# One queue for the step B loads of the first batch, and no early group of the second

## The chip, the cores and the metric

The kernel runs on one core of one Trainium2 chip. The metric is device time of one launch in microseconds: the median of three runs of the kernel before is 1350.76 us (1348.87 to 1351.63). Engines are named as the profile names them: PE (TensorE), PEld (its weight load), DVE (VectorE), ACT (ScalarE), POOL (GpSimd), SP (SyncE, which here only issues DMAs).

## The reference

Each of four batches of 3008 rows by 256 columns goes through a real Fourier transform over the rows, a complex linear map with bias, a soft threshold, and the inverse transform. The 12032 resulting rows then go through a two-layer network whose middle has 2048 columns and a leaky rectifier with a slope per column.

```python
X = np.fft.rfft(x, axis=1)
Yr = Xr @ w_r - Xi @ w_i + b_r
Yi = Xr @ w_i + Xi @ w_r + b_i
Yr = np.sign(Yr) * np.maximum(np.abs(Yr) - lam, 0.0)   # lam = 0.01; Yi likewise
y = np.fft.irfft(Y, n=x.shape[1], axis=1)
h = y @ w_in
out = (np.maximum(h, 0.0) + alpha * np.minimum(h, 0.0)) @ w_out
```

## The kernel before

The transform of 3008 = 47 x 64 rows is made of matmuls with tables, in four steps per batch. Step A (`a_mm`, `a_evac`) multiplies 16 groups of rows with the table `lf_s` into 96 partitions, which are 4 blocks by 2 halves by 12 pairs. Step B (`b_load`, `b_mm`) takes one of the 12 pairs: it gathers 4 partitions per half of step A's result into a tile `bt` of 128 partitions, and multiplies it with rows of the table `rb_s`. The mixing (`m_mm`) multiplies with the split weights `wr_s` and `wi_s`, `m_evac` applies bias and threshold, step C (`c_mm`, `c_evac`) multiplies with `cf_s` and stores to a DRAM tensor `zd`. Step D (`d_load`, `d_step`) reads `zd` back and makes the rows that feed the network (`l1_step`, `l2_step`).

The order of the work is written out by hand; every engine runs its instructions in that order, and a tile is reused only when its last reader is done. The first batch runs alone, ahead of the network:

- The opening: SP loads the rows of the first batch; PE runs step A on them, then four groups (0 to 3) of the second batch (`EARLY = 4`), then 70 matmuls of no use on a tile `idle` (`keep_warm(WARM)`) until step B's data is there. The step B loads of the first batch go from SBUF (`a0_s`) to SBUF and are issued by POOL; those of later batches go from DRAM and are issued by SP. Three `bt` tiles rotate, so the load of pair q needs `b_mm` of pair q - 3 to be done.
- The pair loop, t = 0 to 12: step B of pair t, mixing of pair t - 1, step C of pair t - 3. Beside it, `pump` converts the raw network weights (`cw_s`, loaded by SP in pieces of 512 KB, three buffers) into two parts each, on ACT, DVE and POOL; the table `PT` says how many of its steps an iteration takes. SP also loads table rows (`load_rb`) and, in iterations 5 to 9, rows of the second batch (`a_load`); POOL loads the table `cf_s`.
- The tail (`TAIL`): the last steps of the loop, and ten groups of step A of the second batch (4 to 13) that fill PE while `zd` is written and read back. Then the network's steps begin; the first 48 of them also carry the rest of the conversion and the last two groups (14 and 15) of step A of the second batch, at steps 9 and 15.

The lists `A1_TAGS` and `X1_TAGS` only say in which free tile each early group's result and rows are put. `load_mix` loads the raw mixing weights, `split_mix` splits them in two parts (first part on ACT, rest on POOL), `load_tables` loads `rd_s` and `alpha_s`.

Of the kernel before, what the change touches and what calls it, by code (L numbers as in the profile page):

```python
# [93 lines left out]
def fft_mix_moe(ctx, tc, x, w_r, w_i, b_r, b_i, w_in, w_out, alpha, la, rb, lc, rd, lf, cf, sel, out):  # L94
# [41 lines left out]
    def split(src, hi, lo, e_hi, e_lo):  # L136

        if e_hi is A:
            A.activation(out=hi, in_=src, func=AF.Copy)
        else:  # L140
            e_hi.tensor_copy(out=hi, in_=src)
        e_lo.tensor_tensor(out=lo, in0=src, in1=f(hi), op=ALU.subtract)
# [29 lines left out]
    def load_tables():  # L172
        nc.sync.dma_start(out=rd_s, in_=rd)
        nc.sync.dma_start(out=alpha_s, in_=alpha.rearrange("(k p) -> p k", p=128))
# [33 lines left out]
    def load_mix(*tags):  # L208
        for w, tag in zip((w_r, w_i), tags):
            t = work.tile([128, CT, C], F32, tag=tag, name="wm_f", bufs=1 if tag[1] in "tc" else None)  # L210
            nc.sync.dma_start(out=t, in_=w.rearrange("(k p) f -> p k f", p=128))
            mix_w.append(t)

    def load_rb(n0, n1):
        nc.sync.dma_start(out=rb_s[:, n0:n1], in_=rb[:, n0:n1])
# [9 lines left out]

    def split_mix():
        for t, w in zip(mix_w, mix):
            split(t, w[:, 0], w[:, 1], A, G)
        mix_w.clear()

    def combine_mix():
# [109 lines left out]
    def a_load(b, g):  # L341

        if g == 0:
            ad[b] = dram.tile([NQ, R, C], F32, tag="ad", name=f"ad{b}")
        src = x[b].rearrange("(p r) c -> p r c", r=R)[:, 4 * g:4 * g + 4]
        if b == 0:
            ts = [x_s[:, 4 * g:4 * g + 4]]
        elif b == 1 and g in X1_TAGS:
            tags = X1_TAGS[g]
            ts = [work.tile([NP, 4 // len(tags), C], F32, tag=tag, name="xt", bufs={"Yl": None, "gh": 4}.get(tag, 1))  # L350
                  for tag in tags]
        else:
            ts = [work.tile([NP, 4, C], F32, tag="xt", name="xt")]
        if (b, g) == (0, 0):
            ts = [ts[0][:, 0:2], ts[0][:, 2:4]]
        n = 4 // len(ts)
        for i, t in enumerate(ts):

            for p in ((0, 80), (80, NP)):
                nc.sync.dma_start(out=t[slice(*p)], in_=src[slice(*p), n * i:n * i + n])  # L360
        xt[b, g] = ts
# [50 lines left out]
    def b_load(b, q):  # L412
        t = work.tile([128, 2, C], F32, tag="bt", name="bt", bufs=3)
        if b == 0:
            src = a0_s.rearrange("(w s q) g r c -> q w s (g r) c", w=4, s=2)[q]
        else:
            src = ad[b].rearrange("(w s q) r c -> q w s r c", w=4, s=2)[q]

        for k in range(2):
            (nc.gpsimd if b == 0 else nc.sync).dma_start(out=t[:, k], in_=src[:, k])  # L420
        bt[b, q] = t

    def b_mm(b, q):
# [548 lines left out]
    MM, M2 = 2, 4  # L972
    PAT = [0, 0] + [1] * 46
    NG = R // 2
    EARLY = 4
    FILL = 14
    C0 = 2
    PT = [1, 2, 3, 3, 3, 3, 3, 3, 3, 3, 4, 4]
    TAIL = [['me', 1], ['ce', 3], ['cm', 2], ['cm', 1], ['ce', 2], ['ce', 1], ['d'], ['f', 4], ['e'], ['f', 6]]
    WARM = 70  # L980
    A1_TAGS = ("zst", "zst", "Yt", "Yc", "bt", "bt", "bt", "Xh", "Xl", "Xh", "Xl", "zst", "zst", "Yc")
    X1_TAGS = {4: ("Yl", "Yl"), 5: ("os", "Yt"), 6: ("gh",) * 4}
    idle = const.tile([128, 128], BF16, name="idle")

    def keep_warm(n):
# [4 lines left out]
    with tc.manual_schedule():  # L990
# [5 lines left out]
        for g in range(NG // 2):  # L996
            a_load(0, g)
        load_rb(0, 4)
        for g in range(EARLY // 2):
            a_load(1, g)  # L1000
        load_mix("Yh", "Yh")
        load_rb(4, 12)
        conv_tags.update(v1=("yh", "yl"), ex=("xh", "xh"), lf=("xl", "xl"))
        for _ in range(C0):
            conv_load()
        seq = [(0, g) for g in range(NG)] + [(1, g) for g in range(EARLY)]

        for n, (b, g) in enumerate(seq):
            a_mm(b, g)
            if n >= 1:  # L1010
                a_evac(*seq[n - 1])
            if n == NG:
                for q in range(3):
                    b_load(0, q)
                split_mix()
                bias_parts()
        a_evac(*seq[-1])
        half(0)
        put()
        load_tables()  # L1020
        keep_warm(WARM)

        def run(fn, q, *args):
            if 0 <= q < NPAIR:
                fn(0, q, *args)

        a1 = [EARLY]
        hold = []

        def a_fill(n):  # L1030
# [5 lines left out]
        for t in range(NPAIR + 1):  # L1036
            run(b_mm, t)
            run(b_load, t + 3)
            run(c_evac, t - 4)
            run(b_evac, t)  # L1040
            run(m_evac, t - 2)
            run(m_mm, t - 1, ps_h)
            run(b_evac2, t)
            run(c_mm, t - 3)
            if t < NPAIR:
                pump(PT[min(t, len(PT) - 1)])
            if t in (2, 5):
                load_rb(2 * t + 8, 2 * t + 14)
            if t < 8 and t % 2 == 0:
                load_cf(3 * t, 3 * t + 6)  # L1050
            if 5 <= t < 10:
                a_load(1, t - 3)
            if t == 10:
                half(1)
                conv_m[1] = FT
# [199 lines left out]
```

## Time and profile before

| What | Value |
|---|---|
| median of three runs | 1350.76 us |
| profiled execution, its own time | 1350.56 us |
| its span, first to last instruction | 1348.8 us |
| PE, PEld busy share of the span | 99%, 93% |
| DVE, ACT, POOL | 77%, 56%, 28% |
| granted TensorE clock, mean | 0.999 |

Busy shares are means over the whole span. The change touches only the first 190 us or so: the opening (to 30 us), the pair loop with its tail (30 to 101 us), and the first 48 steps of the network. What an edit there is worth has to be read from these stretches. The profile prints a DMA share (mean busy share of the 16 DMA engines) and GB/s for any stretch; a share can pass 1 where transfers overlap on one engine.

### The profile page before, as it was taken

What the parts mean: (1) busy time and instruction counts of PE and PEld (TensorE: products, weight loads), DVE (VectorE), ACT (ScalarE), POOL (GpSimd) and SP (SyncE); (2) the same over time, 40 slices, a digit from 0 to 9 for tenths busy, and PEclk for the clock granted to TensorE, in tenths of its full rate; (3) what the DMA queues carried; (4) which work ended last, traced back from release to release, by engine and by line L of the source; (5) the groups of instructions that cost most, each with busy time, mean ns of one, the idle gap of its engine ahead of it and who ended that gap; (6) DMA issues with size and microseconds to landing.
All of it is one profiled execution on the core that took longest, in us unless ns stands there. A gap on an engine that the chain in (4) does not pass through costs nothing.

```text
span 1348.8 us, 25138 instructions
## 1 busy us (share of the span) xinstructions
PE 1335.5 (99%) x9200; PEld 1250.7 (93%) x9200; DVE 1034.9 (77%) x1938; ACT 761.0 (56%) x1526; POOL 375.5 (28%) x400
## 2 busy tenths in 40 slices
PE   8999999999999999999999999999999999999998
PEld 4979999999999999999999999999999999999998
DVE  2767856776777777776768888888888888888885
ACT  3566655665566645555555555655555555555653
POOL 3864642222321222222221211121112111211222
PEclk9999999999999999999999999999999999999999
DMA  9974223342333312111110110111011101110001
GB/s 236 251 202 140 81 94 106 105 138 74 98 115 112 111 54 79 53 51 47 36 36 2 40 28 4 37 28 28 6 35 28 28 6 35 29 28 8 22 17 29
DMA packets 88119, 89.67 MB, mean 66 GB/s; under 512 B 42317, under 2 KB 70448, under 8 KB 87995
## 3 DMA queue, kind: packets, MB, share of 16 engines
q1 hardware_dynamic: 79700, 77.02, 20.1%
q0 software_dynamic: 5168, 8.02, 2.2%
q10 hardware_dynamic: 3127, 3.01, 0.7%
q8 instruction: 73, 1.20, 0.4%
q14 instruction: 51, 0.42, 0.1%
HBM read 50.49 MB, written 34.34 MB: 63 GB/s over the span
## 4 chain that ended last, share of the span: by engine, by line
PE 89%; DVE 3%; DMA 3%; issue 2%; ACT 1%; SPq 1%; POOL 0%; ACTq 0%; DVEq 0%; POOLq 0%
PE ps_h L794 24%; PE ps_h L689 13%; PE ps_m L491 6%; PE ps_o L895 6%; PE ps_o L896 6%; PE ps_o L894 6%; PE ps_d L620 4%; PE ps_o L728 3%; PE ps_o L727 3%; PE ps_o L726 3%; PE ps_b L428 2%; PE o_last L727 1%; PE o_last L728 1%; PE o_last L726 1%; PE o_last L894 1%
## 5 line engine op out<-in xcount | busy, mean ns | idle before, releaser
L794 PE MATMUL ps_h<-yh,w 128*128 128x512 f32 (+1 forms) x960 | 315.6, 389 | 0.0
L833 POOL TENSOR_TENSOR l<-t,h 128x512 fp32r<-128x512 f32 x98 | 127.0, 1296 | 496.5 <-ACT h L831 456.9
L794 PEld LDWEIGHTS ps_h<-yh,w 128*128 128x128 f32 x960 | 180.0, 188 | 33.2
L798 DVE SCALAR_TENSOR_TENSOR sq<-sq,beta_s,ps_h 128x512 f32<-128x512 f32 (+1 forms) x240 | 167.9, 732 | 54.5 <-ACT sq L797 53.6
L689 PE MATMUL ps_h<-yh,w 128*128 128x384 f32 (+1 forms) x704 | 207.0, 337 | 1.3 <-DVE q L696 1.3
L794 PE MATMUL ps_h<-yl,w 128*128 128x512 f32 (+1 forms) x480 | 186.2, 388 | 0.0
L696 DVE SCALAR_TENSOR_TENSOR q<-q,beta_s,ps_h 128x384 f32<-128x384 f32 (+1 forms) x192 | 115.1, 600 | 91.8 <-ACT q L695 90.9
L700 ACT ACTIVATE gh<-q 128x384 fp32r<-128x384 f32 (+1 forms) x192 | 99.1, 516 | 148.0 <-DVE q L696 145.3
L701 POOL TENSOR_TENSOR gl<-q,gh 128x384 fp32r<-128x384 f32 (+1 forms) x90 | 96.8, 1075 | 274.9 <-ACT gh L700 265.4
L813 ACT ACTIVATE dh<-sq 128x768 fp32r<-128x768 f32 x112 | 94.8, 846 | 117.8 <-DVE sq L798 75.8
L797 ACT ACTIVATE sq<-ps_h 128x512 f32<-128x512 f32 (+1 forms) x240 | 133.2, 586 | 26.9 <-PE ps_h L794 25.6
L689 PEld LDWEIGHTS ps_h<-yh,w 128*128 128x128 f32 x704 | 129.3, 189 | 4.4 <-DVE q L696 1.3
L695 ACT ACTIVATE q<-ps_h 128x384 f32<-128x384 f32 (+1 forms) x192 | 91.9, 479 | 62.1 <-PE ps_h L689 61.4
L831 ACT ACTIVATE h<-t 128x512 fp32r<-128x512 f32 x98 | 62.0, 633 | 105.2 <-DVE t L829 103.0
L689 PE MATMUL ps_h<-yl,w 128*128 128x384 f32 (+1 forms) x352 | 116.5, 331 | 0.0
L728 PE MATMUL ps_o<-w,gl 128*128 128x256 f32 x384 | 108.0, 281 | 0.6 <-POOL gl L701 0.6
L727 PE MATMUL ps_o<-w,gh 128*128 128x256 f32 x384 | 107.8, 281 | 0.0
L726 PE MATMUL ps_o<-w,gh 128*128 128x256 f32 x384 | 107.7, 280 | 0.0
L794 PEld LDWEIGHTS ps_h<-yl,w 128*128 128x128 f32 x480 | 90.5, 189 | 13.6
L828 DVE TENSOR_TENSOR dl<-sq,dh 128x768 fp32r<-128x768 f32 x98 | 93.4, 953 | 3.9 <-ACT dh L813 3.9
L896 PE MATMUL ps_o<-l,sw_a 128*128 128x256 f32 x294 | 82.0, 279 | 0.0
L894 PE MATMUL ps_o<-h,sw_a 128*128 128x256 f32 x294 | 81.9, 279 | 0.0
(214 smaller groups left out, 3618.5 us busy)
## 6 DMA issues: line engine op xcount, KB each, us to landing
zt<-zd SPq DMA_DIRECT2D x32, 384.0 KB
zd<-zst SPq DMA_DIRECT2D x37, 256.0 KB
ad<-ast SPq DMA_DIRECT2D x48, 192.0 KB
bt<-ad SPq DMA_DIRECT2D x72, 128.0 KB
xt<-in_x SPq DMA_DIRECT2D x21, 320.0 KB
out<-oT SPq DMA_DIRECT2D x152, 32.0 KB
cw_s<-in_moe_w_in SPq DMA_DIRECT2D x8, 512.0 KB
cw_s<-in_moe_w_out SPq DMA_DIRECT2D x8, 512.0 KB
```

The source lines that it names most:

```text
L689: PE.matmul(ps, wi_h[m // FH][:, w, ct, 128 * (m % FH):128 * (m % FH) + 128], a[:, ct, 0:n], start=(k == 0), stop=(k == 3 * CT - 1))
L696: V.scalar_tensor_tensor(out=q, in0=q, scalar=beta_s[:, m:m + 1], in1=ps, op0=ALU.mult, op1=ALU.add)
L700: A.activation(out=hi, in_=q, func=AF.Copy)
L726: PE.matmul(a, hi[:, t], w[:, 0], start=(i, k) in first, stop=False)
L727: PE.matmul(a, hi[:, t], w[:, 1], start=False, stop=False)
L728: PE.matmul(a, lo[:, t], w[:, 0], start=False, stop=(i, k) in last)
L794: PE.matmul(ps, wi_h[m // FH][:, w, ct, 128 * (m % FH):128 * (m % FH) + 128], a[:, ct, 0:w1], start=(k == 0), stop=(k == 3 * CT - 1))
L797: A.activation(out=q[:, j], in_=ps, func=AF.Relu, scale=-1.0)
L798: V.scalar_tensor_tensor(out=q[:, j], in0=q[:, j], scalar=beta_s[:, m:m + 1], in1=ps, op0=ALU.mult, op1=ALU.add)
L833: G.tensor_tensor(out=l24, in0=t24, in1=f(h24), op=ALU.subtract)
L894: PE.matmul(o, wh, gh, start=first, stop=False)
L896: PE.matmul(o, wh, gl, start=False, stop=last)
```

## The change

All step B loads of the first batch are issued by SP. The first three pairs' loads stand right behind step A and, but for one load of table rows, ahead of everything else that SP has to issue; the two first loads of raw weights come after them, `load_tables` in iteration 6. The rest of the mixing weights' split moves from POOL to DVE, behind the bias. No group of the second batch runs in the opening: the tail fills PE with groups 0 to 9 (ten, as before), whose rows are loaded in iterations 7 to 11, and groups 10 to 15 run at steps 9, 15, 21, 27, 33 and 39 of the network. `WARM` goes from 70 to 65, and `PT` from 1 and 2 conversion steps in the first two iterations to 0 and 3 (35 in all, as before).

```diff
     def split_mix():
         for t, w in zip(mix_w, mix):
-            split(t, w[:, 0], w[:, 1], A, G)
+            split(t, w[:, 0], w[:, 1], A, V)
...
         for k in range(2):
-            (nc.gpsimd if b == 0 else nc.sync).dma_start(out=t[:, k], in_=src[:, k])
+            nc.sync.dma_start(out=t[:, k], in_=src[:, k])
...
-    EARLY = 4
-    FILL = 14
+    FILL = 10
...
-    PT = [1, 2, 3, 3, 3, 3, 3, 3, 3, 3, 4, 4]
+    PT = [0, 3, 3, 3, 3, 3, 3, 3, 3, 3, 4, 4]
...
-    WARM = 70
...
+    WARM = 65
...
         for g in range(NG // 2):
             a_load(0, g)
         load_rb(0, 4)
-        for g in range(EARLY // 2):
-            a_load(1, g)
         load_mix("Yh", "Yh")
+        conv_tags.update(v1=("yh", "yl"), ex=("xh", "xh"), lf=("xl", "xl"))
+        for g in range(NG):
+            a_mm(0, g)
+            if g:
+                a_evac(0, g - 1)
+        a_evac(0, NG - 1)
+        b_load(0, 0)
+        b_load(0, 1)
         load_rb(4, 12)
-        conv_tags.update(v1=("yh", "yl"), ex=("xh", "xh"), lf=("xl", "xl"))
+        b_load(0, 2)
         for _ in range(C0):
             conv_load()
-        seq = [(0, g) for g in range(NG)] + [(1, g) for g in range(EARLY)]
-
-        for n, (b, g) in enumerate(seq):
-            a_mm(b, g)
-            if n >= 1:
-                a_evac(*seq[n - 1])
-            if n == NG:
-                for q in range(3):
-                    b_load(0, q)
-                split_mix()
-                bias_parts()
-        a_evac(*seq[-1])
+        bias_parts()
+        split_mix()
         half(0)
-        put()
-        load_tables()
         keep_warm(WARM)
...
-        a1 = [EARLY]
+        a1 = [0]
...
-            if 5 <= t < 10:
-                a_load(1, t - 3)
+            if 7 <= t < 12:
+                a_load(1, t - 7)
+            if t == 6:
+                load_tables()
```

Three places in the order of instructions follow. First SP's queue right behind the rows of the first batch (`wm_f` are the mixing weights, `bt` step B's tiles, `cw_s` raw network weights, `ad` the store of the second batch's step A). Before; four loads of the second batch's rows stand directly ahead of these:

```order
L211 DMA wm_f<-in_w_r 128x2x256
L211 DMA wm_f<-in_w_i 128x2x256
L215 DMA rb_s<-tab_rb 128x1024
L262 DMA cw_s<-in_moe_w_in 128x2x512
L262 DMA cw_s<-in_moe_w_out 128x2x512
L336 DMA ad_160<-ast 96x512 x4
L173 DMA rd_s<-tab_rd 96x94
L174 DMA alpha_s<-in_moe_alpha 128x16x1
```

Of the changed kernel, the same place on SP:

```order
L211 DMA wm_f<-in_w_r 128x2x256
L211 DMA wm_f<-in_w_i 128x2x256
L420 DMA bt<-a_83 128x1x256 x4
L215 DMA rb_s<-tab_rb 128x1024
L420 DMA bt<-a_83 128x1x256 x2
L262 DMA cw_s<-in_moe_w_in 128x2x512
L262 DMA cw_s<-in_moe_w_out 128x2x512
L420 DMA bt<-a_83 128x1x256 x6
```

Twelve half-pair loads `bt<-a` (pairs 0 to 5) now stand among the table rows and raw weights, and the four stores and two tables are gone from here.

Second, SP's queue in the middle of the pair loop, iterations 6 to 8 of the changed kernel (`xt` are rows of the second batch):

```order
L420 DMA bt<-a_83 128x1x256 x2
L262 DMA cw_s<-in_moe_w_out 128x2x512
L173 DMA rd_s<-tab_rd 96x94
L174 DMA alpha_s<-in_moe_alpha 128x16x1
L420 DMA bt<-a_83 128x1x256 x2
L262 DMA cw_s<-in_moe_w_in 128x2x512
L360 DMA xt<-in_x 80x1024
L360 DMA xt<-in_x 14x1024
L420 DMA bt<-a_83 128x1x256 x2
L262 DMA cw_s<-in_moe_w_out 128x2x512
```

The three pairs of `bt` rows here are pairs 9, 10 and 11, and each has raw weights, tables or rows of the second batch ahead of it in one queue; before, SP's queue had no `bt` row in the loop.

Third, POOL's program from the end of the opening into the loop. Before (`wr_s`, `wi_s` are the mixing weights' second parts, `Xh`, `Xl` the sign copies that the mixing waits for):

```order
L994 DMA la_s<-tab_la 94x192
L420 DMA bt<-a_83 128x1x256 x6
L142 ISA
L142 TENSOR_TENSOR wr_s<-wm_f,wr_s 128x512
L142 TENSOR_TENSOR wi_s<-wm_f,wi_s 128x512
L420 DMA bt<-a_83 128x1x256 x2
L457 TENSOR_SCALAR Xh<-Xh 128x4x64
L457 TENSOR_SCALAR Xl<-Xl 128x4x64
```

Of the changed kernel:

```order
L993 DMA la_s<-tab_la 94x192
L457 ISA
L457 TENSOR_SCALAR Xh<-Xh 128x4x64
L457 TENSOR_SCALAR Xl<-Xl 128x4x64
L218 DMA cw_s<-tab_cf 128x768
```

POOL issues no `bt` load any more, and its first work for the loop is the sign copy of pair 0.

## Rows read from the trace of the kernel before

**Rows 1.** Page: chain that ended last, by engine.

```profile
PE 89%; DVE 3%; DMA 3%; issue 2%; ACT 1%; SPq 1%; POOL 0%; ACTq 0%; DVEq 0%; POOLq 0%
```

**Rows 2.** Length; busy of PE, PEld, DVE, ACT, POOL; clock, DMA share, GB/s.

```profile
20.00:30.00 10.00, 7.79 (x78) 5.13 (x78) 1.85 (x5) 3.30 (x6) 6.61 (x8) 1.00 1.07 280
45.00:75.00 30.00, 30.00 (x229) 28.92 (x228) 27.17 (x35) 18.10 (x32) 28.09 (x35) 1.00 0.98 268
75.00:92.00 17.00, 16.24 (x111) 14.30 (x111) 14.19 (x22) 9.92 (x18) 13.13 (x12) 1.00 0.55 172
146.00:170.00 24.00, 22.60 (x165) 21.97 (x164) 20.21 (x30) 13.99 (x32) 14.98 (x12) 1.00 0.26 83
```

**Rows 3.** PE in time, 4 to 101 us: start, length, what, [idle before <-releaser].

```profile
7.33 12.57 PE L389 MATMUL ps_a<-x,lf_s 94*96 94x512 f32 x28 [0.38 <-DMA x<-in_x]
...
25.52 4.07 PE L988 MATMUL ps_idle<-idle 128*128 128x128 bf16 x70
30.42 1.80 PE L428 MATMUL ps_b<-rb_s,bt 128*128 128x128 f32 x12 [0.83 <-issue]
...
33.10 0.71 PE L428 MATMUL ps_b<-rb_s,bt 128*128 128x128 f32 x4 [0.87 <-DMA bt<-a]
33.56 0.47 PE L471 MATMUL ps_m<-bias_p,ones 128*128 128x512 f32 x1
...
36.72 1.05 PE L428 MATMUL ps_b<-rb_s,bt 128*128 128x128 f32 x8
...
40.67 1.05 PE L428 MATMUL ps_b<-rb_s,bt 128*128 128x128 f32 x8
...
79.54 1.05 PE L428 MATMUL ps_b<-rb_s,bt 128*128 128x128 f32 x8
...
91.92 8.76 PE L389 MATMUL ps_a<-xt,lf_s 94*96 94x512 f32 x24
```

**Rows 4.** DVE in time: the last evacuation of step A, first batch.

```profile
19.94 0.69 DVE L404 COPY a<-ps_a 96x512 f32<-96x512 f32 x1 [1.03 <-PE ps_a L389]
```

**Rows 5.** POOL in time: step B loads that it issues.

```profile
21.29 4.11 POOL L420 DMA_DIRECT2D bt<-a  x6 [16.19 <-DVE bias_h L201]
...
31.85 1.37 POOL L420 DMA_DIRECT2D bt<-a  x2 [3.85 <-PE ps_b L428]
```

**Rows 6.** Page: DMA issues, KB each, median us to landing.

```profile
bt<-a POOLq DMA_DIRECT2D x24, 128.0 KB, 7.8
```

**Rows 7.** SP in time, second batch: two step B loads and a store.

```profile
240.95 1.13 SPq L420 DMA_DIRECT2D bt<-ad  x2
243.47 0.39 SPq L336 DMA_DIRECT2D zd<-zst  x1
```

**Rows 8.** Stretches: length, clock, DMA share, GB/s.

```profile
243.50:244.00 0.50, 1.00 0.28 98
244.50:245.00 0.50, 1.00 1.01 365
245.50:246.00 0.50, 1.00 0.27 92
```

**Rows 9.** Stretches of the opening: length, clock, DMA share, GB/s.

```profile
10.00:15.00 5.00, 1.00 1.03 231
22.50:25.50 3.00, 1.00 1.05 398
```

**Rows 10.** SP in time: the scattered small table, and one raw weight load.

```profile
30.37 1.55 SPq L174 DMA_DIRECT2D alpha_s<-in_moe_alpha  x1
...
55.48 0.39 SPq L262 DMA_DIRECT2D cw_s<-in_moe_w_out  x1
```

**Rows 11.** ACT in time: the conversion that waits for that load.

```profile
64.60 0.68 ACT L275 ACTIVATE conv<-cw_s 128x512 f32<-128x512 f32 x1 [0.76 <-DMA cw_s<-in_moe_w_out]
```

**Rows 12.** PE in time around step 9 of the network.

```profile
123.53 0.28 PE L728 MATMUL ps_o<-w,gl 128*128 128x256 f32 x1
123.65 1.02 PE L389 MATMUL ps_a<-xt,lf_s 94*96 94x512 f32 x2
124.11 0.74 PE L689 MATMUL ps_h<-Xh,w 128*128 128x384 f32 x1
124.68 0.33 PE L689 MATMUL ps_h<-Xl,w 128*128 128x384 f32 x1
```

More of the change, by code (lines that the diff above doesn't have):

```diff
@@ L974, in fft_mix_moe @@
     NG = R // 2
-    EARLY = 4
-    FILL = 14
+    FILL = 10
     C0 = 2
-    PT = [1, 2, 3, 3, 3, 3, 3, 3, 3, 3, 4, 4]
+    PT = [0, 3, 3, 3, 3, 3, 3, 3, 3, 3, 4, 4]
     TAIL = [['me', 1], ['ce', 3], ['cm', 2], ['cm', 1], ['ce', 2], ['ce', 1], ['d'], ['f', 4], ['e'], ['f', 6]]
-    WARM = 70
-    A1_TAGS = ("zst", "zst", "Yt", "Yc", "bt", "bt", "bt", "Xh", "Xl", "Xh", "Xl", "zst", "zst", "Yc")
-    X1_TAGS = {4: ("Yl", "Yl"), 5: ("os", "Yt"), 6: ("gh",) * 4}
+    WARM = 65
+    A1_TAGS = ("bt", "bt", "bt", "Xh", "Xl", "Xh", "Xl", "zst", "zst", "Yc")
+    X1_TAGS = {2: ("Yl", "Yl"), 3: ("os", "Yt"), 4: ("gh",) * 4}
     idle = const.tile([128, 128], BF16, name="idle")
```

## The prediction

> **What bounds the kernel now.** I read the page first, for which engine carries the chain that ended last: PE, 89% of it [rows 1]. PE is also busy 99% of the span, so only two things can move the time: matmuls added to or taken from PE where it is full, and stretches where PE waits. Next I asked for the stretches that the change touches [rows 2]. In the opening PE is busy 7.79 of 10 us, and much of that is idle matmuls; in the pair loop it is busy 30.00 of 30; in the early network steps (146 to 170 us) 22.60 of 24. The DMA share beside it is 1.07, 0.98 and 0.26: the transfers are full exactly where the change moves them.
>
> Then PE in order of time [rows 3]. Step A of the first batch ends near 20 us. The four early groups and 70 idle matmuls follow to 29.6, and step B of pair 0 starts at 30.42. Pair 1 is complete only when its load lands, 33.10, and the mixing of pair 0 starts at 33.56. From pair 3 (40.67) to pair 11 (79.54) there are eight intervals in 38.87 us, 4.86 each, with PE full: a loop paced by PE. The tail's fill follows at 91.92. What holds the first pair back is the way from step A's last evacuation, done at 19.94 + 0.69 = 20.63 [rows 4], to the landing: POOL starts to issue at 21.29, takes 4.11 us for six loads [rows 5], and its loads land 7.8 us after issue in the median [rows 6].
>
> **The change part by part.** The sum is made against the profiled execution, 1350.56 us, which is 0.2 below the median of the runs, 1350.76; I treat them as one.
>
> *The four early groups leave the opening.* They stood between step A and the idle matmuls, where PE waited for step B's loads anyway. Alone this saves nothing; it lets PE be ready early: step A ends at 19.9, and 65 idle matmuls at 4.07 / 70 = 58 ns end 3.8 us later, at 23.7.
>
> *The same groups come back at steps 21, 27, 33 and 39.* The row at step 9 prices one: the group starts at 123.65, where the step's first matmul would have started, and the second one, which follows the first by 0.17 in plain steps, comes at 124.68 in place of 123.82. That is 0.86 us each [rows 12], 3.4 for four. PE is not quite full there: 24 - 22.60 = 1.4 us idle from 146 to 170, where two of the four fall [rows 2]. I let half of that hide: 3.4 - 0.7 = +2.7. Bounds: 3.4 if none hides, 2.0 if all does. Their evacuations on ACT (13.99 busy of 24) and their stores and row loads (DMA share 0.26) cost nothing here.
>
> *The split's second part on DVE, the idle count, PT.* DVE is busy 1.85 us between 20 and 30 [rows 2]; two more instructions lie in its idle time. The conversion steps are 35 in both kernels. Nothing, as long as the raw weights come in time; if they don't, ACT and DVE stop in front of them (a rival below).
>
> *POOL loses 24 issues of 0.69 us* (4.11 / 6) [rows 5]. POOL is not what ends the loop's waits. Its first sign copy stood behind the two issues at 31.85; that goes, and only helps pair 0.
>
> *The loads on SP.* This is the part that decides. SP sees step A done at 20.7. How fast does one of these loads move when SP issues it? The first batch's come from SBUF, and no row of before shows that on SP. The nearest rows are the same line for later batches: same shape, from DRAM, issued by SP. Two are issued at 240.95, then a 256 KB store [rows 7]. Away from the store the DMA runs at 98 and 92 GB/s with a share of 0.28 and 0.27; while the store passes it runs at 365 GB/s with a share of 1.01 [rows 8]. A flat share of 0.28 of 16 engines is 4 to 5 engines: these loads use a quarter of the DMA engines, and a pair (262 KB at 97 GB/s) occupies that quarter for 2.7 us. The Trainium skill, "DMA: Bandwidth & Descriptors", section "Why a DMA increments its semaphore by 16 and not by 1", says why: a transfer is spread over the largest number of engines, up to 16, that divides the slowest dimension on both sides, and the source here has four blocks. By that rule the first batch's loads run on four engines as well, the lowest-numbered ones each time, and the trace agrees for the second batch (0.28); a spread over 16 would make a pair cost about 0.7 us, and the loop gain would stay whole.
>
> I take 2.7 us per pair, and the same quarter of the engines each time, which no row shows. Bounds: 0.7 us (262 KB at 365 GB/s), and no bound above that these rows give other than the high sum below.
>
> First pair: 20.7, plus 1.1 to issue [rows 7], plus 2.7, plus some 0.7 until PE sees it: 25.2, against 30.42. Second pair 2.7 later, 27.9; mixing of pair 0 near 28.8, against 33.56 (-4.8). Pair 2 stands behind 512 KB of table rows, pair 3 behind 1 MB of raw weights; at 398 GB/s [rows 9] 512 KB take 1.3. Pair 2: 27.9 + 1.3 + 2.7 = 31.9. Pair 3: 31.9 + 2.6 + 2.7 = 37.2, and 1.0 more for POOL's 384 KB table: 38.2 against 40.67. So of an opening gain of 5 us, 2.4 are left at pair 3.
>
> Then the quarter of the DMA engines is the question. What it has to move from pair 0's to pair 11's load: 12 pairs x 2.7 = 32.4; table rows 1.3 + 1.0 + 1.0 = 3.3; seven raw weight loads x 1.3 = 9.2; four tables from POOL x 1.0 = 4.0; seven stores of step C x 0.72 = 5.0 (262 KB at 365); one load of second-batch rows 1.7 (385 KB at the 231 GB/s of such loads, [rows 9]); the small tables 1.5 (as long as SP was busy with one, [rows 10]). Sum 57.1. From 21.8 that is 78.9, and pair 11 runs at about 79.5: no earlier than now. These are the best rates shown; in the loop the DMA moved only 268 GB/s at a share of 0.98 [rows 2]. With everything but the `bt` loads (24.7 us) stretched by 398 / 268, the sum grows by 12. I take +1.5 for the loop, near the low end, because the heavy stretch of before held loads of second-batch rows that now come mostly behind pair 11. PE needs 8 x 4.86 from pair 3 at 38.2, so without the queue pair 11 would be at 77.1; the loop turns from PE-paced to DMA-paced somewhere in between.
>
> Behind pair 11 the tail is as before: ten groups of fill, the same turn of `zd`. The last second-batch rows come later (iteration 11), but the fill uses them at its end, some 17 us after.
>
> Sum: 1350.56 + 1.5 + 2.7 = 1354.8 us.
>
> **The rivals.**
>
> *A, not slower: the queue keeps pace.* If SP's loads from SBUF run on all engines, or the engines' work overlaps better than my sum, pair 0 starts near 24.6, the mixing near 28, and PE holds its 4.86 from there: the loop ends 5 to 6.5 earlier, less 2.7: about -3.1, 1347.5 us. For it: PE has been the only pacer of the loop, every wait of PE for these loads is in the first two pairs [rows 3], and three tiles of lead are 14 us. The Trainium skill, same page, section "Issuing engines are not separate DMA queues", says that all issuers share the same 16 engines and only issue time is saved by another one; taken alone it would leave the loads' transfer as it was, which is this rival. Against it: 0.28 of the engines for the same line. It decides if the share stays well under 1 in the loop.
>
> *B, much slower: raw weights late.* Raw weights share SP's queue with the pairs. Already now a load issued at 55.48 is waited for by ACT until 64.60, 9.1 us later [rows 10, 11]. ACT and DVE run in order, so a late raw weight holds up the evacuations of steps B and C behind it, and so PE. At two thirds of the high sum (+8) plus 2.7: 1361 us.
>
> *C, about even.* The queue costs what it costs by pair 3 and no more; the loop keeps 2.4 and the moved groups take 2.7: 1350.9 us.
>
> **How the numbers follow.** Within 0.2%, 2.7 us, of the kernel before counts as the same, about what a measurement of it can tell. My forecast has 0.44, with a range of its own of 1351 to 1359 (slower three times in four, else the same); A 0.30 (faster seven times in ten, else the same); C 0.13 (mostly the same); B 0.13 (slower). Faster: 0.21 + 0.01 = 0.22. Slower: 0.33 + 0.13 + 0.02 = 0.48. The same: 0.30. The range runs from inside A, 1347, to just past B, 1363.
>
> **What would show it.** Right: PE starts pair 0 near 25 and mixing near 29; waits of PE for `bt<-a` come up again later in the loop, or of ACT for `cw_s`; DMA rates in the loop fall under 268 GB/s while the loop goes on; pair 11 starts at 79 to 83; four groups `ps_a<-xt` of 0.86 us stand among the steps between 145 and 185. Wrong: intervals of 4.86 all the way from pair 3 with pair 11 before 76 (A), or ACT stopped for several us at L275 (B). I would also be wrong if the granted clock, 1.00 in every stretch above, dropped after the longer pause of PE before pair 1, or if the moved groups vanished in waits of the steps.

## The result, and the profile after

The changed kernel takes 1364.1 us (median of 5 runs, 1363.04 to 1364.98), against 1350.76 for the kernel before (5 runs beside them): ratio 1.010, 95% interval 1.0085 to 1.0115, or +13.3 us. The forecast was +4.2 (1354.8), with a range up to 1363. The direction was right; the time lies just outside the range. The profiled execution took 1363.37 us, its span 1361.6.

The chain that ended last of the changed kernel [answers to rows 1], and the stretches of [rows 2] (length; busy of PE, PEld, DVE, ACT, POOL; clock, DMA share, GB/s):

```profile
PE 92%; DMA 3%; DVE 1%; ACT 1%; SPq 1%; issue 1%; ACTq 0%
```

```profile
20.00:30.00 10.00, 6.58 (x79) 5.79 (x77) 3.80 (x8) 1.43 (x3) 1.36 (x3) 0.84 0.41 110
45.00:75.00 30.00, 27.19 (x187) 25.86 (x185) 20.14 (x27) 13.94 (x25) 16.34 (x18) 0.89 0.68 204
75.00:92.00 17.00, 15.02 (x100) 14.03 (x99) 13.60 (x19) 8.96 (x16) 10.35 (x11) 0.90 0.76 226
146.00:170.00 24.00, 23.73 (x166) 22.31 (x165) 19.44 (x29) 14.89 (x33) 15.52 (x13) 1.00 0.27 77
```

PE's share of the chain rose, and that misleads: a PE at half clock is busy too. The stretch to read is 45 to 75 us. Before, PE was busy 30.00 of 30 at a clock of 1.00 and ran 229 matmuls; now 27.19 at 0.89, with 187 matmuls. The DMA engines did not get fuller in exchange: 204 GB/s in place of 268. In the opening, too, the DMA is half empty: 110 GB/s against 280.

PE in order of time, changed kernel [answers to rows 3]:

```profile
19.86 3.79 PE L987 MATMUL ps_idle<-idle 128*128 128x128 bf16 x65
24.40 0.68 PE L428 MATMUL ps_b<-rb_s,bt 128*128 128x128 f32 x4 [0.75 <-DMA bt<-a]
...
28.00 1.19 PE L428 MATMUL ps_b<-rb_s,bt 128*128 128x128 f32 x4 [1.36 <-DVE Xl L453]
29.66 1.22 PE L428 MATMUL ps_b<-rb_s,bt 128*128 128x128 f32 x4 [0.46 <-DMA bt<-a]
...
40.29 0.68 PE L428 MATMUL ps_b<-rb_s,bt 128*128 128x128 f32 x4 [0.34 <-DMA bt<-a]
...
52.67 1.16 PE L428 MATMUL ps_b<-rb_s,bt 128*128 128x128 f32 x8 [1.53 <-ACT zst L570]
61.73 1.05 PE L428 MATMUL ps_b<-rb_s,bt 128*128 128x128 f32 x8
...
89.95 1.05 PE L428 MATMUL ps_b<-rb_s,bt 128*128 128x128 f32 x8
...
102.46 8.76 PE L389 MATMUL ps_a<-xt,lf_s 94*96 94x512 f32 x24
```

The rows at 28.00 and 29.66 are the two halves of pair 1, those at 52.67 and 61.73 pairs 5 and 6. Pair 0 starts 6.0 us earlier than before (24.40 for 30.42). By pair 3 nothing is left of that (40.29 for 40.67). Pair 11 is 10.4 late (89.95 for 79.54), the tail's fill 10.5 (102.46 for 91.92). The span grew by 12.8, so the other 2.3 come later, where the moved groups stand.

SP and then ACT of the changed kernel show why:

```profile
20.83 3.48 SPq L420 DMA_DIRECT2D bt<-a  x4
...
27.60 1.05 SPq L262 DMA_DIRECT2D cw_s<-in_moe_w_in  x1
28.69 0.58 SPq L262 DMA_DIRECT2D cw_s<-in_moe_w_out  x1
29.38 11.02 SPq L420 DMA_DIRECT2D bt<-a  x6
40.45 1.36 SPq L262 DMA_DIRECT2D cw_s<-in_moe_w_in  x1
```

```profile
37.38 0.66 ACT L275 ACTIVATE conv<-cw_s 128x512 f32<-128x512 f32 x1 [5.86 <-DMA cw_s<-in_moe_w_in]
...
51.48 0.66 ACT L275 ACTIVATE conv<-cw_s 128x512 f32<-128x512 f32 x1 [7.83 <-DMA cw_s<-in_moe_w_in]
```

Issuing is not free: six half-pair loads hold SP for 11.02 us, and the third raw weight behind them, issued at 31.96 before, goes out at 40.45. ACT, which runs in order, stands at L275 for 5.86 us (for the first raw weight, issued at 27.60) and again for 7.83 (for the third); the evacuations behind it stand too, and then PE. That is the mechanism of rival B. Five stretches complete it, for two of them with the line of the profile that counts the DMA packets:

```profile
16.00:20.00 4.00, 4.00 (x13) 1.54 (x12) 1.38 (x2) 1.75 (x4) 0.00 (x0) 1.00 0.59 168
20.00:25.00 5.00, 4.25 (x70) 4.00 (x67) 3.10 (x7) 0.83 (x2) 0.00 (x0) 1.00 0.16 51
...
37.00:38.00 1.00, 1.00 (x10) 1.00 (x9) 0.00 (x0) 0.62 (x2) 0.00 (x0) 1.00 0.27 104
DMA packets 51, 0.10 MB, mean 104 GB/s; under 512 B 0, under 2 KB 0, under 8 KB 51
...
38.00:41.00 3.00, 2.63 (x21) 2.27 (x19) 2.72 (x6) 1.67 (x4) 1.11 (x2) 1.00 0.27 93
DMA packets 279, 0.28 MB, mean 93 GB/s; under 512 B 11, under 2 KB 275, under 8 KB 279
...
55.00:60.00 5.00, 4.89 (x22) 4.79 (x23) 4.86 (x7) 2.80 (x6) 4.15 (x5) 0.50 0.68 184
```

From 20 to 25 us the DMA engines are almost idle. From 38 to 41 almost nothing but step B loads moves (packets of about 1 KB, 0.28 MB in 279), and the share stands at 0.27, the quarter that [rows 8] promised. From 37 to 38 no packet under 2 KB moves. What runs there are packets of 2 KB (0.10 MB in 51), rows of the first two raw weights (512 words of 4 bytes), and they too run at a share of 0.27. SP had issued both weights by 29.3. So the first stop of ACT, which ends at 37.38, is not explained by SP's blocked issue alone: the last part of a wide load that stands behind narrow ones moves as slowly as they do. And after PE's stop near 51 to 55 us the granted clock is 0.50, the lower of its two levels (1.2 GHz).

### The profile page after: what moved, and what is told of

The parts are those of the page before. It is cut to its first block, busy times and chain, and to the rows that moved or that the text cites. A ratio compares the mean times of both kernels' runs of the same rounds, so it can differ in the third digit from the quotient of the medians.

```text
span 1361.6 us, 25113 instructions
## 1 busy us (share of the span) xinstructions
PE 1342.8 (99%) x9195; PEld 1257.6 (92%) x9195; DVE 1034.6 (76%) x1940; ACT 760.4 (56%) x1526; POOL 356.1 (26%) x374
## 4 chain that ended last, share of the span: by engine, by line
PE 92%; DMA 3%; DVE 1%; ACT 1%; SPq 1%; issue 1%; ACTq 0%
PE ps_h L794 24%; PE ps_h L689 14%; PE ps_m L491 6%; PE ps_o L895 6%; PE ps_o L896 6%; PE ps_o L894 6%; PE ps_d L620 4%; PE ps_o L728 3%; PE ps_o L727 3%; PE ps_o L726 3%; PE ps_b L428 3%; PE ps_a L389 2%; PE o_last L727 1%; PE o_last L728 1%; PE o_last L726 1%; PE o_last L894 1%
## 5 line engine op out<-in xcount | busy, mean ns | idle before, releaser
L794 PEld LDWEIGHTS ps_h<-yl,w 128*128 128x128 f32 x480 | 90.6, 189 | 13.5
```

The lines of the kernel that those rows point to most:

```text
L794: PE.matmul(ps, wi_h[m // FH][:, w, ct, 128 * (m % FH):128 * (m % FH) + 128], a[:, ct, 0:w1], start=(k == 0), stop=(k == 3 * CT - 1))
```

## The experiments

T1 was: on SP, step B loads take a quarter of the DMA engines one after another, raw weights queue behind them, and ACT stops. The rivals named in the expectations are other homes for the 13 us. "Before" in these comparisons was 1350.5 to 1350.7 us.

**1. All first-batch step B loads back on POOL, the rest of the change kept.**

```diff
-            nc.sync.dma_start(out=t[:, k], in_=src[:, k])
+            (nc.gpsimd if b == 0 else nc.sync).dma_start(out=t[:, k], in_=src[:, k])
```

> The changed kernel with one word undone: the first batch's step B loads go back to POOL; everything else of the change stays. Theory 1 (SP's narrow step B loads hold up its queue, raw weights come late, ACT waits in front of them, PE pauses and its clock falls): the pair loop is paced by PE again, 4.8 to 4.9 us from pair 3 to pair 11, ACT's waits for raw weights fall from 23.6 us to under 3, the granted clock is 1.00 after 35 us, and the fill starts at 85 to 92 us in place of 102.4; with 2.3 us for the moved groups the time is 1346 to 1354 us. Rival 2 (the moved groups, the later rows of the second batch or the other split are what costs): the loop stays irregular and the time over 1360 us.

1353.15 us, ratio 1.0022 (1.0012 to 1.0032). One line takes back 11 of the 13.3 us; the rest of the change costs +2.65. Pair 11 is at 79.35 and there is no stop at L275. Its stretches from 16 to 25 us show what SP does when no step B load blocks it:

```profile
16.00:20.00 4.00, 4.00 (x12) 1.50 (x11) 1.37 (x2) 1.75 (x4) 0.00 (x0) 1.00 1.05 339
20.00:25.00 5.00, 3.69 (x66) 3.52 (x63) 3.11 (x7) 0.87 (x2) 3.56 (x6) 1.00 1.04 386
```

It issues three raw weights and two loads of table rows by 18.5 us. The DMA moves 4 x 339 + 5 x 386 = 3286 KB here (GB/s times us); in the changed kernel 4 x 168 + 5 x 51 = 927 KB. And it shows how the same loads move when POOL issues them and nothing else does (`q0` is POOL's queue):

```profile
26.00:28.00 2.00, 0.00 (x0) 0.00 (x0) 0.00 (x0) 0.00 (x0) 0.00 (x0) 0.79 1.02 121
q0 software_dynamic: 389, 0.24, 101.7%
```

They are not much faster, 121 GB/s against 93, but the share is 1.02 in place of 0.27. That fits loads that are not kept to a quarter of the engines; since the share also counts transfers that overlap, it does not prove it.

**2. Each half-pair load cut in four, one per source block, to spread it over more engines.**

```diff
-            nc.sync.dma_start(out=t[:, k], in_=src[:, k])
+            for w in range(4) if b == 0 else (slice(4),):
+                o = t[32 * w:32 * w + 32, k] if b == 0 else t[:, k]
+                nc.sync.dma_start(out=o, in_=src[w:w + 1, k] if b == 0 else src[:, k])
```

> The changed kernel with each half of a step B load of the first batch cut in four on SP, one per block of the source, so that the slowest dimension is 32 rows on both sides: 96 loads of 32 KB in place of 24 of 128 KB. Theory 1, narrow transfers: the DMA share no longer stands flat at 0.27 while they run, SP is through with them sooner, ACT's waits for raw weights fall under 8 us (from 23.6), time 1346 to 1356 us. Rival 3 (it is the one queue and its order, not the width): SP issues four times as many loads in the same queue, raw weights come as late or later, time 1364 us or more.

1384.46 us, ratio 1.025 (1.023 to 1.027): 20 us worse. The share did rise, the rate fell:

```profile
22.00:32.00 10.00, 4.59 (x40) 3.72 (x37) 1.76 (x3) 0.60 (x1) 1.36 (x3) 0.76 0.73 51
```

Each of these loads reads one source partition, and there are four times as many; which of the two makes them slow was not separated. A high DMA share is no proof of a high rate.

**3. The one word alone, in the kernel before.**

```diff
-            (nc.gpsimd if b == 0 else nc.sync).dma_start(out=t[:, k], in_=src[:, k])
+            nc.sync.dma_start(out=t[:, k], in_=src[:, k])
```

> The kernel before with one word changed: the first batch's step B loads go to SP, everything else as before (early groups, rows, order; the first two raw weights stand ahead of the loads). Theory 1: loop disturbed as in the changed kernel, ACT waits for raw weights 10 us or more, the granted clock falls in the loop, time 1357 to 1368 us. Rival 2: within 3 us of the kernel before.

1366.82 us, ratio 1.0119 (1.0104 to 1.0134), +16.3. The queue alone reproduces the loss; the rest of the change is not needed for it. Its opening gains nothing either, since the early groups and 70 idle matmuls still fill PE to 30 us. Nor is the clock needed. Pair 8 of this run, then pair 8 of the kernel before, and the clock of this run up to there:

```profile
70.93 1.05 PE L428 MATMUL ps_b<-rb_s,bt 128*128 128x128 f32 x8
```

```profile
65.04 1.05 PE L428 MATMUL ps_b<-rb_s,bt 128*128 128x128 f32 x8
```

```profile
20.00:75.00 55.00, 44.76 (x348) 38.95 (x347) 24.92 (x39) 21.71 (x38) 22.28 (x28) 1.00 0.73 213
```

5.9 us are lost by then, at a granted clock of 1.00 throughout.

**4. Is the clock the cause? Forty idle matmuls behind each of the first two pairs.**

```diff
             run(b_mm, t)
+            if t < 2:
+                keep_warm(40)
```

> The changed kernel with 40 idle matmuls behind step B of pairs 0 and 1, where PE pauses for loads (2.3 us each at the full clock). If the fall of the granted clock between 26.7 and 33.7 us is a cost of its own, it goes: the stretch 27 to 33 us is at 1.00, mixing of pair 0 takes 2.8 us in place of 4.5, pair 3 starts some 2 us earlier; but the raw weights are as late, so the loop's later stop in front of the fourth conversion takes most of it back: time 1361 to 1364 us. If the loads alone set the pace in the opening, pair 3 starts at 40.3 as before and the time is 1364 or up to 4 more.

1363.54 us, ratio 1.0096 (1.0081 to 1.0111): nothing gained. The stretch from 30 to 45 us, and pair 3:

```profile
30.00:45.00 15.00, 14.32 (x140) 14.00 (x139) 5.84 (x11) 5.27 (x9) 4.63 (x8) 1.00 0.63 174
```

```profile
40.12 0.65 PE L428 MATMUL ps_b<-rb_s,bt 128*128 128x128 f32 x4
```

The clock is at its upper level throughout this stretch (1.00, 2.4 GHz; 0.88 on the mean in the changed kernel), and pair 3 comes at 40.12 in place of 40.29. From 25 to 30 us it still is 0.66. Four more us at the upper level, from 29 to 33, bring pair 3 no sooner: there the loads set the pace, and that part of the early fall costs nothing by itself.

**5. Pairs 0 to 2 on SP, pairs 3 to 11 on POOL.**

```diff
-            nc.sync.dma_start(out=t[:, k], in_=src[:, k])
+            (nc.gpsimd if b == 0 and q > 2 else nc.sync).dma_start(out=t[:, k], in_=src[:, k])
```

> Step B loads of pairs 0 to 2 on SP, ahead of the raw weights, as in the changed kernel; those of pairs 3 to 11 on POOL. T1 (SP's loads gain 5 us in the opening and lose in the loop because raw weights stand behind them in one queue): mixing of pair 0 starts near 30.5 us, as after the change, pair 3 before 39 us, no wait of ACT for a raw weight over 2 us, PE-paced pairs of 4.85 us from there to pair 11 at 77 to 78.5; time 1350.5 to 1352.5. Rival (most of the lost time comes from the opening itself, from the three pairs that SP loads there, and from the clock falling after them): pair 3 at 40 us or later and a time above the 1353.15 us of all loads on POOL.

1358.0 us, ratio 1.0052 (1.0039 to 1.0065). Neither: the loop is PE-paced from pair 3 on (45.27 us; 4.85 each to pair 11), but it starts late. PE waits for the second half of pair 2, and ACT still stops once, longer than ever:

```profile
40.12 0.71 PE L428 MATMUL ps_b<-rb_s,bt 128*128 128x128 f32 x4 [4.20 <-DMA bt<-a]
```

```profile
42.28 0.68 ACT L275 ACTIVATE conv<-cw_s 128x512 f32<-128x512 f32 x1 [10.87 <-DMA cw_s<-in_moe_w_in]
```

ACT waits for the first raw weight, which SP issued at 27.57 behind pairs 0 to 2 alone. The DMA was left idle before, and much is asked for at once from 27 us on (from 35 to 40 us the share is 1.07). T1 explains only a part. T3 was added, and runs 9 and 10 test it: SP waits for step A at the head of its queue while the wide loads behind it could have moved.

**6. Raw weights of the loop issued by POOL, step B loads all on SP.**

```diff
-        nc.sync.dma_start(out=raw.rearrange(...
+        (nc.gpsimd if conv_m[1] < FT else nc.sync).dma_start(out=raw.rearrange(...
```

> The changed kernel with the raw weights of the pair loop issued by POOL; all step B loads stay on SP. T1 (what costs is that raw weights stand behind step B loads in SP's queue): the third raw weight is issued before 35 us in place of 40.45, ACT's waits at L275 fall from 19.4 us to under 5, PE's pause at 51 to 55 us and the clock of 0.50 behind it go; time 1352 to 1357. Rival (the quarter of the DMA engines that a step B load runs on is itself the bound, whichever queue the weights use): pair 11 stays near 90 us, PE waits for bt grow in place of ACT's waits; time 1361 or more.

1369.34 us, ratio 1.0129 (1.011 to 1.0148), and of no use for the question: POOL issued the first two raw weights at 5.05 us, ahead of the later of SP's rows of the first batch, step A starved, and the clock fell in the opening:

```profile
15.00:20.00 5.00, 3.76 (x6) 1.22 (x5) 0.69 (x1) 0.87 (x2) 0.00 (x0) 0.65 1.04 240
```

**7. A third raw weight in the opening, ahead of the six loads.**

```diff
-    C0 = 2
+    C0 = 3
```

> The changed kernel with three raw weights in place of two loaded in the opening, so that the third stands ahead of the six loads for pairs 3 to 5 on SP. T1 (one late raw weight stops ACT, then DVE and PE, and the clock falls): the third weight lands before 40 us in place of 51.5, the wait of 7.8 us at L275 near 51 us and the clock of 0.50 after it go; the pairs 2 to 4 come 1 to 2 us later; of the 10.5 us that the loop loses, 4 to 8 come back: 1356 to 1360. Rival (the total of bytes on SP's queue sets the pace of the loop, not the place of one load): the wait moves to a later weight, time within 2 us of 1364.

1363.76 us, ratio 1.0097 (1.0081 to 1.0112): the rival's number. The stop at 51 us is gone; ACT's next stop is the next weight, at 56.26:

```profile
56.26 0.68 ACT L275 ACTIVATE conv<-cw_s 128x512 f32<-128x512 f32 x1 [5.58 <-DMA cw_s<-in_moe_w_out]
```

So one late load by itself is not what costs the time: what is moved ahead in a full queue pushes back something else.

**8. As run 6, but the first two raw weights stay on SP.**

```diff
+        (nc.gpsimd if C0 < conv_m[0] and conv_m[1] < FT else nc.sync).dma_start(out=raw.rearrange(...
```

> The changed kernel with the raw weights of the pair loop, from the third on, issued by POOL; the first two stay where they were, so that the opening is that of the changed kernel. T1 (the step B loads hold up the raw weights behind them in SP's queue): the third weight lands 4 us earlier or more than at 51.5, ACT's longest wait at L275 falls from 7.8 us to under 4, time 1354 to 1360. Rival (in the opening too little is moved, and the loop then has too much to move, in whatever queue): ACT's waits stay within 4 us of 22.4 us in sum, time 1362 to 1366.

1366.33 us, ratio 1.0115 (1.0101 to 1.0129): no gain. POOL came to the third weight only at 41.17, behind its own work (SP: 40.45), and it landed by 49.03, 2.4 us sooner than in the changed kernel. ACT's waits for weights fell from 23.6 to 17.1 us, but now ACT also waits for step B loads (5.3 us), and six of these hold SP for 13.23 us. That is between the two signs that were set, and since the weights were issued no sooner, the run does not show what an early issue on another queue would give.

**9. Table rows and the two first raw weights ahead of step B on SP, as they stood before; all step B loads on SP.**

```diff
+        load_rb(4, 12)
+        for _ in range(C0):
+            conv_load()
         b_load(0, 0)
         b_load(0, 1)
-        load_rb(4, 12)
         b_load(0, 2)
-        for _ in range(C0):
-            conv_load()
```

> The changed kernel with the table rows and the two first raw weights ahead of step B's loads of pairs 0 to 2 on SP, as they stood before; everything else as changed. T3 (in the changed kernel the DMA engines stand nearly idle from 16 to 25 us, share 0.46 and then 0.14 to 0.16, because SP waits there for step A with the wide loads behind it; the 1.5 MB not moved there are missing in the loop): DMA share over 0.5 from 16 to 21 us, pair 0 at 24.3 to 26, pair 3 by 38 us, the wait of 5.9 us at L275 near 37 us gone, and half or more of the loop's 10.5 us back: 1354 to 1359. T1 alone (the third raw weight behind six loads of step B): the wait of 7.8 us near 51 us stays as it is, time 1360 to 1364.

1358.31 us, ratio 1.0054 (1.0038 to 1.0069): 5.8 us better than the changed kernel, by order alone. The idle time of the DMA is used (367 GB/s from 16 to 20 us, 168 before the edit), and the first stop of ACT is gone. What is left starts behind twelve loads:

```profile
16.00:20.00 4.00, 4.00 (x15) 1.68 (x15) 1.49 (x3) 1.75 (x4) 0.00 (x0) 1.00 1.06 367
```

```profile
20.65 15.14 SPq L420 DMA_DIRECT2D bt<-a  x12
35.83 0.53 SPq L262 DMA_DIRECT2D cw_s<-in_moe_w_in  x1
```

**10. Both: that order, and pairs 3 to 11 on POOL** (the edits of runs 9 and 5).

> The same order, raw weights and table rows ahead of step B's loads of pairs 0 to 2 on SP, and the loads of pairs 3 to 11 on POOL. T1 and T3 together (both causes away): opening like the changed kernel's, pair 3 before 39 us, no wait of ACT for raw weights over 2 us, pairs 4.85 us apart, pair 11 at 76 to 78.5; time 1348 to 1351.5. Rival (PE-paced pairs start no earlier because POOL's loads of pairs 3 and 4 are late in the full DMA engines, or the clock falls in PE's pauses): pair 4 after 45 us, time over 1352.5.

1351.23 us (11 runs), ratio 1.0005 (0.9996 to 1.0014): the same as before. No stop of ACT at L275; PE busy 50.00 of 50 us from 30 to 80; pair 11 at 77.61, 1.9 us earlier than before, which the moved groups then take back.

```profile
30.00:80.00 50.00, 50.00 (x376) 48.60 (x375) 39.58 (x55) 27.75 (x48) 40.95 (x52) 0.96 0.87 230
```

**11. As run 9, but pairs 3 to 11 issued by ACT.**

```diff
-            nc.sync.dma_start(out=t[:, k], in_=src[:, k])
+            (nc.scalar if b == 0 and q > 2 else nc.sync).dma_start(out=t[:, k], in_=src[:, k])
```

> Raw weights and table rows first, as in the run before that had all step B loads on SP (1358.3 us, against 1351.2 with pairs 3 to 11 on POOL); now the loads of pairs 3 to 11 are issued by ACT. ACT pays the issues, 18 of at least 0.5 us, in stretches where it is busy about half the time. If the 7.1 us of the loop come from the wide loads standing in one queue with the narrow ones (T1 in the form of throughput: the queue moves only 89 to 105 GB/s while a step B load is at its head), two queues run side by side: no stretch of the loop stays at a DMA share of 0.27 for long while wide loads wait, SP issues raw weights without stops of 5 us, time 1351 to 1354.5. If instead the quarter of the DMA engines on which these loads run is itself full, or the issue blocks ACT as it blocked SP, the time is 1357 us or more.

1359.87 us, ratio 1.007 (1.0056 to 1.0083): no better than on SP. But the time is lost elsewhere. SP issues its weights almost without stops now (0.37 us each from 41 to 56 us), and ACT's waits for them are down to 2.9 us in sum (16.0 in run 9); in their place ACT waits 13.0 us for step B's loads, and 9.0 in front of step C's evacuations (`zst`) by its own issues. The issue holds up the engine that computes:

```profile
55.60 3.30 ACTq L420 DMA_DIRECT2D bt<-a  x1
58.94 0.60 ACT L570 ACTIVATE zst<-ps_c 128x512 f32<-128x512 f32 x1 [3.54 <-issue]
```

**12. As run 10, with idle matmuls in front of the halves of pairs 0 and 1.**

```diff
+            for _ in range((12, 12, 12, 4)[2 * q + s] if b == 0 and q < 2 else 0):
+                PE.matmul(ps[:, s, 0], idle, idle, start=True, stop=True)
```

> Raw weights first, pairs 0 to 2 on SP, pairs 3 to 11 on POOL, and 40 idle matmuls (58 ns each at full clock, 2.3 us) in front of the halves of pairs 0 and 1, where PE waits for loads for 3 us in sum. If the clock of 0.58 from 30 to 35 us is what keeps that kernel from the gain of its opening (PE busy 5 us of 5 at 0.58 is about 2 us of lost work), the granted clock from 25 to 35 us is above 0.9, pair 3 starts near 37.5 in place of 38.96, pair 11 near 76 in place of 77.6: time 1349 to 1350.3, below both kernels. If the loads set the pace there, as they did in the changed kernel with idle matmuls, pair 3 stays at 38.5 to 39 and the time at 1351 to 1352.

1349.95 us (11 runs), ratio 0.9998 (0.9989 to 1.0007): the lowest median of all, 0.65 us under before, but not told apart from it. The clock is 1.00 from 25 us on, and pair 3 waits for its load instead:

```profile
30.00:35.00 5.00, 4.95 (x41) 4.71 (x40) 1.54 (x3) 1.83 (x4) 3.26 (x6) 1.00 1.03 235
```

```profile
38.57 1.13 PE L430 MATMUL ps_b<-rb_s,bt 128*128 128x128 f32 x8 [1.31 <-DMA bt<-a]
```

**13 and 14. The suspected cost by itself.** To run 10, extra copies on SP at the places of the loads of pairs 3 to 11, into DRAM that nobody reads: first 18 of the loads' own shape, then 27 wide ones with 12% more bytes.

```diff
+        if b == 0 and q > 2:
+            d = dram.tile([2, 4, 32, 2 * C], F32, tag=f"du{q}", name="du")
+            for k in range(2):
+                nc.sync.dma_start(out=d[k, :, :, 0:C], in_=src[:, k])
```

```diff
+        if b == 0 and q > 2:
+            d = dram.tile([3, 96, C], F32, tag=f"du{q}", name="du")
+            for k in range(3):
+                nc.sync.dma_start(out=d[k], in_=a0_s[:, q, k % 2])
```

> The kernel with raw weights first and pairs 3 to 11 on POOL (1351.2 us), and beside it 18 extra copies on SP, where the changed kernel has its step B loads of pairs 3 to 11: same source, same shape (4 partitions to 128 rows of 1 KB, 128 KB each), but into DRAM that nobody reads. No data is late by its own load. If the loss of pairs 3 to 11 on SP (7.1 us) is made by what a transfer of this shape does to the queue and to the wide loads behind it, these copies cost as much: 1356 to 1361, with ACT stopping at L275 for raw weights and flat stretches at a DMA share of 0.27. If the loss came from the step B data itself being late (PE's wait for bt), they cost under 2 us: 1350.5 to 1353.

> The same kernel with extra copies of the same bytes and a little more (27 of 96 KB, 2.65 MB against 2.36) at the same places on SP, from 96 partitions in place of 4, into DRAM that nobody reads. If the narrow shape is the cause, these cost little: 1351 to 1354, and no stop of ACT over 3 us. If the bytes on SP's queue are the cause whatever their shape, they cost as much as the narrow copies, 1356 or more.

Narrow: 1372.37 us, ratio 1.0158 (1.0139 to 1.0177), 21.1 over run 10. Wide: 1356.55, ratio 1.0045 (1.003 to 1.006), 5.3 over it. Both cost more than expected; the wide ones, too, reach the 1356 us that were the sign for bytes whatever their shape. So bytes alone cost something in a loop whose DMA is nearly full (a share of 0.87 in run 10); but nearly the same bytes cost four times as much from 4 partitions as from 96. From 30 to 80 us, narrow and then wide:

```profile
30.00:80.00 50.00, 42.60 (x297) 39.45 (x296) 29.17 (x42) 20.46 (x36) 32.84 (x45) 0.94 0.79 214
```

```profile
30.00:80.00 50.00, 47.87 (x355) 46.19 (x354) 36.76 (x51) 26.36 (x46) 38.93 (x49) 0.96 0.97 273
```

ACT's waits for raw weights are 26.7 us in sum in the narrow one (up to 6.2 each), in the wide one 5.4 for the weights of the first layer (up to 2.3). No narrow copy is waited for by anyone, so what costs is what the shape does to the other work; the largest part seen is the wide loads behind it in the queue.

**The sum of the runs.** Four steps lead from before to the changed kernel: the rest of the change with the loads on POOL, +2.65 (run 1); pairs 0 to 2 on SP behind the raw weights, 1351.23 - 1353.15 = -1.9 (run 10); the raw weights and table rows put behind them, 1358.0 - 1351.23 = +6.8 (run 5); pairs 3 to 11 on SP, 1364.1 - 1358.0 = +6.1. The steps share their ends, so that they add up (to 13.6, for 13.3 measured with other runs beside it) is no test; they give the size of each. In the other order of the last two, the queue costs +7.1 (1358.31 - 1351.23) and the order +5.8: the two hardly depend on each other. The 16.3 us of run 3 are more than both queue steps; there SP's queue also holds the early groups' stores and rows, and no run separates that.

## Why the prediction was wrong in size

- *Early groups leave the opening, the split on DVE, the idle count: 0.* Right as far as shown: pair 0 starts at 24.40 (25.2 forecast), PE waiting only for its load.
- *Moved groups: +2.7, bounds 2.0 to 3.4.* Right. Run 1 has them without the queue: +2.65 in the time. The first of them, at step 21 of the changed kernel, has the price of [rows 12]: the step's second matmul starts 160.41 - 159.37 = 1.04 us after its first would have, less the 0.17 of plain steps 0.87, against 0.86:

```profile
159.37 1.02 PE L389 MATMUL ps_a<-xt,lf_s 94*96 94x512 f32 x2
...
160.41 0.33 PE L689 MATMUL ps_h<-Xl,w 128*128 128x384 f32 x1
```

- *A pair on SP takes a quarter of the engines for 2.7 us.* Right: a share of 0.27 at 93 GB/s (38 to 41 us; 2.8 us a pair), where 0.28 at 97 was taken from loads out of DRAM.
- *Opening: pair 3 at 38.2, 2.4 us gained.* Wrong by 2.1: pair 3 at 40.29. The sum had nothing for a DMA left idle from 20 to 25 us at a share of 0.16, after which raw weights, table rows and a POOL table come at once. Run 9, which only fills that time, has pair 3 at 37.41.
- *Loop: +1.5, chosen near the low end of a sum that ran to +12.* **This is the step that failed**: it was +10.5. The total was nearly complete (by the sizes of the loads its list is some 12.0 MB, and 13.5 MB moved from 21.8 us to the start of pair 11), the rate was wrong. The high end stretched the wide loads by the loop's 268 GB/s, and I took the low end since the second-batch rows leave the loop's middle. They did leave, and the rate fell all the same, to 204 GB/s: narrow transfers at the head of the queue hold a quarter of the engines and idle the rest, the last part of the wide loads behind them moves at that rate too (37 to 38 us), and meanwhile SP's issue stops. An estimate from the rows: the 2.36 MB that run 1 moved from 16 to 25 us and the changed kernel did not, at 204 GB/s, are 11.6 us. That is near what the loop lost, but the missing bytes are not the whole: runs 9 and 10 moved nearly the same in these 9 us (2373 and 2467 KB) and end 7.1 us apart. That the direction came out right does not speak for this term: the moved groups alone give it.
- *The second mistake is in the form of the sum.* It put one deadline at its end, pair 11's load at 79.5. The queue has a deadline at every raw weight, and the first is at 31.5 us, where ACT stops in the changed kernel. A stop there passes on to DVE and PE and is not made up later, since PE has no spare time in the loop. Rival B had this mechanism, at 13%, and priced the queue's part at +8.
- *The clock.* The text said it would be wrong if the clock fell after the longer pause of PE before pair 1. It did (0.50 from 27 to 33 us), and again after ACT's stops (0.50 from 55 to 60). Run 4 shows that most of the early fall costs nothing while the loads set the pace, and run 3 loses 5.9 us by pair 8 without any fall. What the later falls cost by themselves was not separated.

On two rules that the prediction weighed. With one order of loads, pairs 3 to 11 gave 1351.2 us on POOL, 1358.3 on SP and 1359.9 on ACT. The Trainium skill ("DMA: Bandwidth & Descriptors", section "Issuing engines are not separate DMA queues") says that another issuing engine saves only the time of issuing, which is usually small beside the transfer. Here the measurement decides against it in two points: issuing was not small (11.02 us for six loads), and the transfers themselves differ in the share that they hold (0.27 from SP, 1.02 from POOL). How much of the 7 to 9 us is issue time is open. The Trainium skill, same page, section "Why a DMA increments its semaphore by 16 and not by 1", offers a reason that would fit: loads from SP and ACT always take the lowest-numbered engines, those from GpSimd a group that moves on from load to load. The two shares fit it, and so do the raw weights that finish at 0.27 behind SP's loads. But no row here shows which engines a load took, so that this is what parts POOL from SP and ACT is argued, not shown.

Open: how much of the 6 to 7 us for pairs 3 to 11 is SP's blocked issue, and how much the full quarter of the engines. The traces show both at work: the first raw weight of the changed kernel came 9.8 us after its issue, the third was issued 8.5 us later than before. Run 11 took the weights out of the narrow loads' queue, and they were hardly late any more; but it put the issue on ACT, so its time does not separate the two.

## What to carry to other kernels

Give every transfer on a shared queue its own deadline, and look first for a load at the head that waits for a computation while wide loads stand behind it: moving those ahead was worth 6 to 7 us here. Price narrow transfers by how long they hold their part of the DMA engines and by what stands behind them in their queue, not by their bytes alone, and let the issuing engine's own time (11 us for six) count as a cost to all that it issues after. When a sum has a high end that comes from a measured rate, a reason to leave it must itself rest on a measured rate.

## What was not expected of the hardware

- Issuing a DMA can hold the issuing engine for microseconds: six half-pair loads held SP for 11.02 us, a single one held ACT for 3.30.
- Loads that read one partition each (32 KB) kept the DMA share at 0.73 and moved 51 GB/s; the loads from 4 partitions moved 93 at a share of 0.27 when SP issued them, and 121 at a share of 1.02 when POOL did.
- Wide loads behind such narrow ones in SP's queue ended as slowly: packets of 2 KB alone, at 104 GB/s and a share of 0.27 (37 to 38 us of the changed kernel).
- Extra copies that nobody reads cost 21.1 us in the narrow shape and 5.3 in the wide one, with 12% more bytes in the latter.
